# Token blocks of 512 instead of 448, and streaming tiles laid on multiples of 128 bytes

## The chip, the core and the metric

The kernel runs on one core of a Trainium2 chip. The metric is the time of one execution in microseconds of the device. TensorE (PE) multiplies matrices into PSUM; ScalarE (ACT) and VectorE (DVE) work between PSUM and the on-chip memory SBUF; SyncE (SP) issues transfers.

## What is computed

An attention over 49 agents, then two feed-forward layers, for 12480 tokens of 128 channels, in fp32:

```python
def _attn_ref(q, k, v, agents):
    scale = 1.0 / np.sqrt(q.shape[-1])
    def sm(a, b):
        s = scale * (a @ b.transpose(0, 2, 1))
        ...                                     # softmax over the last axis
    agent_v = sm(agents, k) @ v
    return sm(q, agents) @ agent_v              # q is (1, 12480, 128), agents (1, 49, 128)

def _moe_ref(x, w_in, w_out, s, b):             # w_in (128, 2048), w_out (2048, 128)
    r = np.maximum(x @ w_in, 0.0)
    return (s * (r * r) + b) @ w_out

def _moe2_ref(x, w_in, w_out):                  # the second layer, same shapes
    h = np.maximum(x @ w_in, 0.0)
    return h * h @ w_out
```

## The kernel before

**Two halves of each number.** To keep fp32 accuracy with the fast fp32r matmuls, each operand is held as a high half and a low half (names end in `h` and `l`), and a product is two or three matmuls: low by high, high by low, high by high. The weights are decoded into halves on ACT and DVE (`w_decode`, in small portions that `fill` deals out; the table `FILL_L` says how many portions each of the first 22 steps gets).

**The head** (0 to 77 us) reads k and v, forms the agents' values, and folds them into the first layer's weights: `M` is agent values times `w_in` (`m_piece`, L385, 512 columns at a time). L507 streams `wo` past a matrix of ones to get its column sums (`colsum`, 512 columns).

**The loop.** The tokens are cut into blocks. `cut(4, BP)` with `BP = 112` makes 27 blocks of 4 × 112 = 448 tokens and one of 384. A block takes 8 steps (`NPR`), each for two of the 16 chunks of the hidden 2048. A step holds 22 matmuls of one block's width: `up1` (L595) 4, X by `M`; `up2` (L605) 6, y by `wi2`; `down` (L621) 6 and 6, g by `wo` and by `wo2`. The four parts belong to different steps of different blocks (`LAG = 2`, `L2 = 11` steps later), so that PE always has something to do while ACT squares the hidden values (L584, L585 in `hidden`) and DVE splits them into `gh` and `gl` (L125, L126 in `split`). A matmul has two operands in SBUF: the weights, 128 columns that are loaded (PEld) while the matmul ahead still runs, and the streaming tile, one column after another (X, `yh`, `yl`, `gh`, `gl`, and for the scores `qh`, `ql`).

**Around the loop.** Once in a block, in fixed steps of it (`QS`), the queries of the next block are turned into X: `q_scores_T` (L214, two matmuls that stream `ql` and `qh` past `aS`), `q_back` (L229, two transposes), exponent, norm, and `q_stack` (L260, two transposes). q itself is loaded three blocks ahead through SP's queue: the first three blocks directly, later ones channel by channel or, every fourth (`TURN`), in 32 × 32 squares that DVE turns. The result leaves through the same queue.

**Where tiles lie.** Nothing sets an address outright. Pools take space in the order in which they are opened, tiles in a pool in the order of the code, each rounded up to 32 bytes of a partition. `const` holds `ident`, `aT`, `s_sb`, the weights, then the small tiles, a filler `apart` and X; the pool `qp` follows with q, `mx`, `e`, `sm`; the other pools after it. In the built programs this gives (byte of a partition, modulo 512; all weights of a kind, and all buffers of a tile, have the same):

| streaming tile, weights | before: tile, weights | distance modulo 512 | after: tile, weights | distance |
|---|---|---|---|---|
| X, M (L595) | 384, 416 | 480 | 128, 128 | 0 |
| y, wi2 (L605) and g, wo, wo2 (L621) | 64, 416 | 160 | 128, 128 | 0 |
| ql, aS (L214) | 64, 416 | 160 | 128, 128 | 0 |
| qh, aS (L214) | 384, 416 | 480 | 128, 128 | 0 |
| wo, ones_r (L507) | 416, 384 | 32 | 128, 128 | 0 |
| M, av (L385) | 416, 416 | 0 | 128, 128 | 0 |

Of the kernel before, what the change touches and what calls it, by code (L numbers as in the profile page):

```python
# [9 lines left out]
F32 = mybir.dt.float32  # L10
F32R = mybir.dt.float32r
# [4 lines left out]
AX = mybir.AxisListType  # L16

P = 128
BP = 112
SQ = 32  # L20
LAG = 2
WC = 512
# [23 lines left out]
def tile_agent_attention_two_moe(  # L46
# [15 lines left out]
    _, N, C = q.shape  # L62
# [5 lines left out]
    GAP = 64  # L68
    KS = GAP + NA

    def cut(rows, most=P):

        pieces, t = [], 0
        while N - t >= rows * most:
            pieces.append((t, most, rows))
            t += rows * most
        if t < N:
            left = N - t
            p = next(x for x in range(min(most, left), 0, -1) if left % x == 0 and left // x <= rows)
            pieces.append((t, p, left // p))  # L80
        return pieces

    blocks = cut(4, BP)
    kblocks = cut(8)
    NT = sum(j for _, _, j in kblocks)

# [5 lines left out]

    const = ctx.enter_context(tc.tile_pool(name="const", bufs=1))
    qp = ctx.enter_context(tc.tile_pool(name="qp", bufs=2))
    ps_h = ctx.enter_context(tc.tile_pool(name="ps_h", bufs=2, space=bass.MemoryType.PSUM))
    ps_y = ctx.enter_context(tc.tile_pool(name="ps_y", bufs=1, space=bass.MemoryType.PSUM))
    ps_m = ctx.enter_context(tc.tile_pool(name="ps_m", bufs=1, space=bass.MemoryType.PSUM))
# [2 lines left out]
    def small(name):  # L100

        flip[0] = (flip[0] + 1) % (flip[1] + 1)
        return ps_m.tile([P, 512], F32, tag=f"m{flip[0]}", name=name)

    ident = const.tile([P, P], F32, name="ident")
    aT = const.tile([P, GAP], F32, name="aT")
    s_sb = const.tile([P, 1], F32, name="s_sb")
    M = [const.tile([P, DFF], F32R, name=f"M{x}") for x in "hl"]
    wo = [const.tile([P, NCH, C], F32R, name=f"wo{x}") for x in "hl"]
    wi2 = [const.tile([P, DFF], F32R, name=f"wi2{x}") for x in "hl"]  # L110
# [2 lines left out]
    sTs = [const.tile([KS, 256], F32, name=f"sT{i}") for i in range(2)]  # L113
    aS = const.tile([P, P], F32R, name="aS")
    av = [const.tile([P, P], F32R, name=f"av{x}") for x in "hl"]
    b_sb = const.tile([P, 1], F32, name="b_sb")
    y1_bias = const.tile([P, 1], F32, name="y1_bias")
    const.tile([P, 104], F32, name="apart")
    Xs = [const.tile([P, 512], F32R, name=f"X{i}") for i in range(2)]
    ones_r = const.tile([P, P], F32R, name="ones_r")  # L120
    halves = (0, slice(0, NA)), (1, slice(GAP, KS))

    def split(dst, src, eng_lo, copy=nc.vector.tensor_copy):
# [5 lines left out]
    q_raw, qT, q_sT, q_e, q_st, X = {}, {}, {}, {}, {}, {}  # L129

    def tokens_of(x, t):

        t0, p, j = blocks[t]
        return x[t0:t0 + p * j, :].rearrange("(j p) c -> p j c", j=j)

    def squares_of(x, t, a, e, g):

        t0 = blocks[t][0]
        return x[t0 + a:t0 + e, g * SQ:(g + 1) * SQ].rearrange("(b p) c -> p b c", p=SQ)

    def squares(x, a, e, g):

        return x[g * SQ:(g + 1) * SQ, a:e].rearrange("p (b c) -> p b c", c=SQ)

    def q_load(t):
        t0, p, j = blocks[t]
        q_raw[t] = qp.tile([P, 512], F32, tag="q_raw", name="q_raw", bufs=3)
        if t < DIRECT:
            nc.sync.dma_start(out=q_raw[t].rearrange("p (j c) -> p j c", c=C)[:p, :j], in_=tokens_of(q, t))
        else:  # L150
            if t % TURN:
                with nc.allow_non_contiguous_dma(reason="channels on the partitions"):
                    nc.sync.dma_start(out=q_raw[t][:, :p * j], in_=q[t0:t0 + p * j, :].rearrange("t c -> c t"))
            else:
                for g in range(P // SQ):
                    nc.sync.dma_start(out=squares(q_raw[t], 0, p * j, g), in_=squares_of(q, t, 0, p * j, g))
# [8 lines left out]
    def q_transpose(t):  # L165
        _, p, j = blocks[t]
        n = p * j
        raw = q_raw.pop(t)
        if t < DIRECT:
            ps = small("ps_q")  # L170
            for i in range(j):
                nc.tensor.transpose(
                    out=ps[:, i * p:(i + 1) * p], in_=raw[:p, i * C:(i + 1) * C], identity=ident[:p, :p]
                )
            qT[t] = qp.tile([P, 512], F32, tag="qh", name="qT")
            nc.scalar.copy(qT[t][:, :n], ps[:, :n])
        else:
            hi = qp.tile([P, 512], F32R, tag="qh", name="qh")
            lo = qp.tile([P, 512], F32R, tag="ql", name="ql")
            nc.scalar.copy(hi[:, :n], raw[:, :n])  # L180
            qT[t] = (hi, lo, raw)

# [205 lines left out]
    with tc.manual_schedule():  # L388

        with tc.tile_pool(name="pre", bufs=1) as pre, tc.tile_pool(name="kp", bufs=2) as kp:  # L390
# [74 lines left out]
            for g in range(NG + 1):  # L465
                if g < NG:
                    k_transpose(g)
                if g and g + KB - 1 < NG:
                    k_load(g + KB - 1)
                if g == 2:  # L470
                    nc.scalar.dma_start(out=s_sb, in_=s.partition_broadcast(P))
                    nc.scalar.dma_start(out=b_sb, in_=b.partition_broadcast(P))
                if g == 9:
                    q_load(0)
                    q_load(1)
                v_upto(min(g - KB, VB))
                fill(FILL_K[g])
                if g:
                    k_scores(g - 1)
                if g > 2:  # L480
                    k_max(g - 2)

            k_max(NG - 1)
            mxk = pre.tile([P, NA], F32, name="mxk")
            nc.vector.reduce_max(mxk, mxa.rearrange("p j n -> p n j"), axis=AX.X)
            q_transpose(0)
            fill(FILL_T)
            ps = small("ps_mt")
# [3 lines left out]
            dm = pre.tile([NA, NA], F32, name="dm")  # L492
            nc.vector.tensor_scalar_mul(dm, ident[:NA, :NA], mt)
            q_transpose(1)
            fill(FILL_T)
            ps = small("ps_mb")
# [10 lines left out]
                    nc.tensor.matmul(out=ps_cs, lhsT=ones_r, rhs=w, start=(n == 0), stop=(n == 2 * NW - 1))  # L507

            def set_bias():
                x = qp.tile([P, 512], F32, tag="ql", name="cs")  # L510
                nc.vector.tensor_tensor(
                    out=x.rearrange("p (m c) -> p m c", c=C),
                    in0=ps_cs.rearrange("p (m c) -> p m c", c=C),
                    in1=ident.rearrange("p (m c) -> p m c", m=1).to_broadcast([P, 512 // C, C]),
                    op=ALU.mult,
                )
                nc.vector.reduce_sum(y1_bias, x, axis=AX.X)
                nc.vector.tensor_mul(y1_bias, y1_bias, b_sb)
# [128 lines left out]
        for st in range(total + L2 + LAG + 1):  # L647
            t, i = divmod(st, NPR)
            if t + 1 < NB and i == QS[2]:
                q_exp(t + 1)  # L650
            if st == NPR:
                set_bias()
# [10 lines left out]
            if t < NB:  # L663
                up1(t, i)
                if i == 0:
                    for u, far in ((t + 2, t + 2 < DIRECT), (t + 3, DIRECT <= t + 3 < NB)):
                        if far:
                            q_load(u)
                if t + 1 < NB:
                    if t + 2 < NB and i == NPR - 2:  # L670
                        q_turn(t + 2)
                    elif t + 2 < NB and i == NPR - 1:
                        q_transpose(t + 2)
                    if i == QS[0]:
                        (q_scores if t + 1 < DIRECT else q_scores_T)(t + 1)
                    elif i == QS[1] and t + 1 >= DIRECT:
                        q_back(t + 1)
                    elif i == QS[3]:
                        q_norm(t + 1)
                    elif i == QS[4]:  # L680
                        q_stack(t + 1)
            t, i = divmod(st - L2, NPR)
            if 0 <= t < NB:
                up2(t, i)
            t, i = divmod(st - LAG, NPR)
# [4 lines left out]
            t, i = divmod(st - L2 - LAG, NPR)  # L690
# [34 lines left out]
```

## Time and profile before

| | us |
|---|---|
| median of 3 runs | 1103.91 (1103.86 to 1104.81) |
| the profiled execution | 1104.85 |
| its span, first to last instruction | 1102.9 |
| PE busy in it | 1084.2 (98%) |
| DVE busy | 954.4 (87%) |
| ACT busy | 952.8 (86%) |

The rows further down are from that one profiled execution. Matmuls overlap in the pipeline, so the duration of one is longer than the distance between two starts, and the end is modelled; distances of starts are read from the timeline and from the chain of waits.

### The profile page before, as it was taken

How to read it: one execution, taken by the hardware profiler on the slowest of the kernel's cores; microseconds unless marked ns; L12 is line 12 of the kernel's file. 1: busy time of each engine (PE TensorE's matmuls, PEld its weight loads, DVE VectorE, ACT ScalarE, POOL GpSimd, SP SyncE). 2: the span in 40 equal slices, each digit the busy share in tenths (PEclk: the TensorE clock that was granted, in tenths of full speed). 3: DMA queues.
4: the chain of work that ended last, by engine and by line, in shares of the span. 5: the costliest groups of instructions: out<-in, count | busy, mean ns of one | idle time of the engine just before them, and what ended most of it. 6: DMA issues, size and time to landing. Idle time of an engine off the chain costs nothing.

```text
span 1102.9 us, 15258 instructions
## 1 busy us (share of the span) xinstructions
PE 1084.2 (98%) x5651; PEld 1010.8 (92%) x5651; DVE 954.4 (87%) x1413; ACT 952.8 (86%) x1201; POOL 12.5 (1%) x36
## 2 busy tenths in 40 slices
PE   8997999999999999999999999999999999999998
PEld 8886999999999999999999999999999999999997
DVE  5889888888888888988889888888888888888876
ACT  5659998989898889988988988898989898889876
POOL 2010000000000000000000000000000000000000
PEclk9899999999999999999999999999999999999999
DMA  9999949983999909999099992799973999800001
GB/s 342 262 195 15 8 11 8 16 20 11 9 14 15 21 9 8 15 16 13 11 15 15 15 8 18 13 15 8 15 20 12 8 15 15 12 9 1 9 9 16
DMA packets 1163202, 34.95 MB, mean 32 GB/s; under 512 B 1145575, under 2 KB 1159544, under 8 KB 1163128
## 3 DMA queue, kind: packets, MB, share of 16 engines
q1 hardware_dynamic: 1160224, 27.57, 104.0%
q0 software_dynamic: 1728, 6.29, 1.8%
q8 instruction: 44, 0.72, 0.4%
q14 instruction: 30, 0.25, 0.2%
q10 hardware_dynamic: 1176, 0.12, 0.1%
HBM read 27.58 MB, written 6.39 MB: 31 GB/s over the span
## 4 chain that ended last, share of the span: by engine, by line
PE 89%; DVE 3%; ACT 2%; issue 1%; DMA 1%; DVEq 0%; ACTq 0%
PE ps_y L621 47%; PE ps_h L605 24%; PE ps_h L595 16%; PE ps_sT L214 1%; DMA raw<-in_moe_w_out_dram 1%; ACT r L584 1%; DVE gl L126 1%; ACT r L585 1%; PE ps_x L260 0%; PE ps_b L229 0%; DVE gh L125 0%; DVE z L313 0%; DVE x L308 0%; DVE S L523 0%; DVE ex L316 0%
## 5 line engine op out<-in xcount | busy, mean ns | idle before, releaser
L126 DVE TENSOR_TENSOR gl<-r,gh 128x896 fp32r<-128x896 f32 (+2 forms) x450 | 487.6, 1083 | 17.1 <-ACT gh L125 1.8
L584 ACT ACTIVATE r<-ps_h 128x896 f32<-128x896 f32 (+2 forms) x450 | 408.5, 908 | 73.4 <-PE ps_h L595 36.3
L585 ACT ACTIVATE r<-r 128x896 f32<-128x896 f32 (+2 forms) x450 | 427.0, 949 | 14.3
L125 DVE CAST gh<-r 128x896 fp32r<-128x896 f32 (+2 forms) x445 | 275.2, 618 | 101.4 <-ACT r L585 98.3
L605 PE MATMUL ps_h<-yh,wi2l 128*128 128x448 f32 (+1 forms) x448 | 167.3, 374 | 0.2 <-ACT r L584 0.2
L595 PE MATMUL ps_h<-X,Ml 128*128 128x448 f32 (+1 forms) x448 | 163.7, 365 | 2.2 <-DVE X L271 1.3
L595 PE MATMUL ps_h<-X,Mh 128*128 128x448 f32 (+1 forms) x448 | 164.1, 366 | 0.0
L621 PE MATMUL ps_y<-gh,wol 128*128 128x448 f32 (+1 forms) x448 | 162.6, 363 | 1.1 <-ACT y L629 1.1
L621 PE MATMUL ps_y<-gl,woh 128*128 128x448 f32 (+1 forms) x448 | 162.3, 362 | 0.6 <-DVE gl L126 0.6
L621 PE MATMUL ps_y<-gl,wo2h 128*128 128x448 f32 (+1 forms) x448 | 162.2, 362 | 0.1
L605 PE MATMUL ps_h<-yl,wi2h 128*128 128x448 f32 (+1 forms) x448 | 162.2, 362 | 0.0
L621 PE MATMUL ps_y<-gh,woh 128*128 128x448 f32 (+1 forms) x448 | 162.1, 362 | 0.0
L605 PE MATMUL ps_h<-yh,wi2h 128*128 128x448 f32 (+1 forms) x448 | 162.0, 362 | 0.0
L621 PE MATMUL ps_y<-gh,wo2l 128*128 128x448 f32 (+1 forms) x448 | 162.0, 362 | 0.0
L621 PE MATMUL ps_y<-gh,wo2h 128*128 128x448 f32 (+1 forms) x448 | 161.9, 361 | 0.0
L595 PEld LDWEIGHTS ps_h<-X,Ml 128*128 128x128 f32 x448 | 84.4, 188 | 9.2 <-issue 2.9
L621 PEld LDWEIGHTS ps_y<-gh,wol 128*128 128x128 f32 x448 | 84.4, 188 | 7.0 <-ACT y L629 1.4
L595 PEld LDWEIGHTS ps_h<-X,Mh 128*128 128x128 f32 x448 | 84.4, 188 | 6.7
L621 PEld LDWEIGHTS ps_y<-gl,woh 128*128 128x128 f32 x448 | 84.2, 188 | 6.4 <-DVE gl L126 0.9
L605 PEld LDWEIGHTS ps_h<-yh,wi2h 128*128 128x128 f32 x448 | 84.1, 188 | 6.2
L605 PEld LDWEIGHTS ps_h<-yh,wi2l 128*128 128x128 f32 x448 | 84.1, 188 | 6.1 <-ACT r L584 0.6
L621 PEld LDWEIGHTS ps_y<-gl,wo2h 128*128 128x128 f32 x448 | 84.1, 188 | 5.8 <-DVE gl L126 0.6
(122 smaller groups left out, 941.6 us busy)
## 6 DMA issues: line engine op xcount, KB each, us to landing
kraw<-in_k_dram SPq DMA_DIRECT2D x12, 512.0 KB, 12.0
v<-in_v_dram SPq DMA_DIRECT2D x12, 512.0 KB, 8.5
out_dram<-o SPq DMA_DIRECT2D x108, 56.0 KB, 1.9
q_raw<-in_q_dram SPq DMA_DIRECT2D x21, 224.0 KB, 36.3
raw<-in_moe_w_out_dram POOLq DMA_DIRECT2D x8, 512.0 KB, 8.6
raw<-in_moe_w_in_dram SPq DMA_DIRECT2D x4, 512.0 KB, 8.8
raw<-in_moe_w_in_dram POOLq DMA_DIRECT2D x4, 512.0 KB, 7.5
q_raw<-in_q_dram SPq DMA_DIRECT2D x24, 56.0 KB, 2.2
```

The lines of the kernel that those rows point to most:

```text
L125: copy(dst[0], src)
L126: eng_lo.tensor_tensor(out=dst[1], in0=src, in1=dst[0].bitcast(F32), op=ALU.subtract)
L214: nc.tensor.matmul(out=ps[:, :n], lhsT=aS, rhs=x[z][:, :n], start=(z == 1), stop=(z == 0))
L584: nc.scalar.activation(r[:, c, :n], ps[:, c, :n], AF.Relu)
L585: nc.scalar.activation(r[:, c, :n], r[:, c, :n], AF.Square)
L595: nc.tensor.matmul(out=ps[:, c, :n], lhsT=M[z][:, sl], rhs=X[t], start=(z == 1), stop=(z == 0))
L605: nc.tensor.matmul(out=ps[:, c, :n], lhsT=w[:, sl], rhs=y[:, :n], start=(z == 0), stop=(z == 2))
L621: nc.tensor.matmul(out=py[t][:, :n], lhsT=wz[:, m], rhs=g[:, c, :n], start=(m == 0 and z == 0), stop=(m == NCH - 1 and z == 2),)
```

## The change

Blocks become as wide as a matmul allows, 4 × 128 = 512 tokens: 23 of them, then one of 384 and one of 320 (`TAIL`). The tiles are laid anew: the small ones go behind the weights, X and the ones ahead of them, another filler follows, and q's tiles get a pool of their own, `qs`, behind the small tiles of `qp`. No other code changes; lines move by up to 5 (L595 becomes L600, L605 L610, L621 L626).

```diff
-BP = 112
+TAIL = [96, 80]
...
-    blocks = cut(4, BP)
+    blocks, left = [], N
+    for p in [P] * (N // (4 * P) - 1) + TAIL:
+        blocks.append((N - left, p, 4))
+        left -= 4 * p
...
     qp = ctx.enter_context(tc.tile_pool(name="qp", bufs=2))
+    qs = ctx.enter_context(tc.tile_pool(name="qs", bufs=2))
...
     ident = const.tile([P, P], F32, name="ident")
-    aT = const.tile([P, GAP], F32, name="aT")
-    s_sb = const.tile([P, 1], F32, name="s_sb")
     M = [const.tile([P, DFF], F32R, name=f"M{x}") for x in "hl"]
...
     av = [const.tile([P, P], F32R, name=f"av{x}") for x in "hl"]
+    ones_r = const.tile([P, P], F32R, name="ones_r")
+    Xs = [const.tile([P, 512], F32R, name=f"X{i}") for i in range(2)]
+    aT = const.tile([P, GAP], F32, name="aT")
+    s_sb = const.tile([P, 1], F32, name="s_sb")
     b_sb = const.tile([P, 1], F32, name="b_sb")
     y1_bias = const.tile([P, 1], F32, name="y1_bias")
-    const.tile([P, 104], F32, name="apart")
-    Xs = [const.tile([P, 512], F32R, name=f"X{i}") for i in range(2)]
-    ones_r = const.tile([P, P], F32R, name="ones_r")
+    const.tile([P, 120], F32, name="apart0")
...
-        q_raw[t] = qp.tile([P, 512], F32, tag="q_raw", name="q_raw", bufs=3)
+        q_raw[t] = qs.tile([P, 512], F32, tag="q_raw", name="q_raw", bufs=3)
...
-            hi = qp.tile([P, 512], F32R, tag="qh", name="qh")
-            lo = qp.tile([P, 512], F32R, tag="ql", name="ql")
+            hi = qs.tile([P, 512], F32R, tag="qh", name="qh")
+            lo = qs.tile([P, 512], F32R, tag="ql", name="ql")
```

In a steady step PE has, before (numbers behind a name are buffers; the shape is that of the output):

```order
L595 MATMUL ps_h_2251<-X_91,Ml 128x448
L595 MATMUL ps_h_2251<-X_91,Mh 128x448
L605 MATMUL ps_h_2268<-yh,wi2l 128x448
L605 MATMUL ps_h_2268<-yl,wi2h 128x448
L605 MATMUL ps_h_2268<-yh,wi2h 128x448
```

and with the change, at the same place:

```order
L600 MATMUL ps_h_2254<-X_90,Ml 128x512
L600 MATMUL ps_h_2254<-X_90,Mh 128x512
L610 MATMUL ps_h_2271<-yh,wi2l 128x512
L610 MATMUL ps_h_2271<-yl,wi2h 128x512
L610 MATMUL ps_h_2271<-yh,wi2h 128x512
```

The sequence is the same and each matmul is 64 columns wider. Where the last block enters the loop, PE has before:

```order
L595 MATMUL ps_h_10247<-X_92,Ml 128x384
L595 MATMUL ps_h_10247<-X_92,Mh 128x384
L605 MATMUL ps_h_10259<-yh,wi2l 128x448
L605 MATMUL ps_h_10259<-yl,wi2h 128x448
L605 MATMUL ps_h_10259<-yh,wi2h 128x448
```

and with the change:

```order
L600 MATMUL ps_h_9318<-X_90,Ml 128x320
L600 MATMUL ps_h_9318<-X_90,Mh 128x320
L610 MATMUL ps_h_9330<-yh,wi2l 128x384
L610 MATMUL ps_h_9330<-yl,wi2h 128x384
L610 MATMUL ps_h_9330<-yh,wi2h 128x384
```

Two narrower blocks run through the end where one did, and the very last is 320 wide.

## Rows read from the trace of the kernel before

**Rows 1.** The page's busy line: engine, busy us, share of the span, instructions.

```profile
PE 1084.2 (98%) x5651; PEld 1010.8 (92%) x5651; DVE 954.4 (87%) x1413; ACT 952.8 (86%) x1201; POOL 12.5 (1%) x36
```

**Rows 2.** Ramp and loop: length, busy us by engine (instructions), clock, DMA share.

```profile
77.40:118.00 40.60, 34.12 (x163) 29.37 (x164) 37.15 (x63) 37.36 (x49) 0.00 (x0) 0.96 1.58 13
118.00:1040.00 922.00, 922.00 (x4637) 859.61 (x4637) 813.85 (x1155) 825.99 (x1019) 0.00 (x0) 1.00 1.11 13
```

**Rows 3.** Chain of waits in order of time, one step: start, us, what.

```profile
995.13 0.82 PE ps_h L595 x4
995.95 1.20 PE ps_h L605 x6
997.15 2.40 PE ps_y L621 x12
999.55 0.82 PE ps_h L595 x4
```

**Rows 4.** The same chain in the last block and the tail.

```profile
1084.00 1.04 PE ps_y L621 x6
1085.04 1.04 PE ps_h L605 x6
...
1092.36 0.50 ACT r L584
...
1097.46 0.63 PE ps_y L621 x2
```

**Rows 5.** PE's groups by form: count, busy us, mean ns, idle before.

```profile
L595 PE MATMUL ps_h<-X,Mh 128*128 128x448 f32 x432 | 158.7, 367 | 0.0
...
L621 PE MATMUL ps_y<-gh,wo2h 128*128 128x448 f32 x432 | 156.6, 362 | 0.0
...
L214 PE MATMUL ps_sT<-ql,aS 128*128 128x448 f32 x24 | 8.8, 367 | 0.0
L214 PE MATMUL ps_sT<-qh,aS 128*128 128x448 f32 x24 | 8.8, 367 | 0.0
```

**Rows 6.** L385, 512 columns: durations min/median/max in ns, first and last start.

```profile
L385 PE MATMUL ps_M<-Ml,avh x4: 389/434/487, 75.1 to 85.8; 128*128 128x512 f32 x4
...
L385 PE MATMUL ps_M<-Mh,avl x4: 389/394/607, 75.3 to 86.1; 128*128 128x512 f32 x4
...
L385 PE MATMUL ps_M<-Mh,avh x4: 388/393/628, 75.5 to 86.5; 128*128 128x512 f32 x4
```

**Rows 7.** L507, 512 columns, the same view.

```profile
L507 PE MATMUL ps_cs<-wol,ones_r x4: 393/398/398, 73.0 to 74.8; 128*128 128x512 f32 x4
```

**Rows 8.** Timeline of PE, L385: start, us, what.

```profile
75.06 0.39 PE L385 MATMUL ps_M<-Ml,avh 128*128 128x512 f32 x1
...
75.75 0.39 PE L385 MATMUL ps_M<-Ml,avh 128*128 128x512 f32 x1
...
76.21 0.39 PE L385 MATMUL ps_M<-Mh,avh 128*128 128x512 f32 x1
```

**Rows 9.** Timeline of PE at the two transposes of a block.

```profile
538.86 0.36 PE L229 MATMUL ps_b<-ident,sT 113*112 113x113 f32 x2
538.99 0.45 PE L605 MATMUL ps_h<-yh,wi2l 128*128 128x448 f32 x1
539.27 0.37 PE L605 MATMUL ps_h<-yl,wi2h 128*128 128x448 f32 x1
...
991.15 0.36 PE L260 MATMUL ps_x<-ident,stack 112*113 112x112 f32 x2
...
991.57 0.36 PE L605 MATMUL ps_h<-yl,wi2h 128*128 128x448 f32 x1
```

**Rows 10.** PE's waits in the ramp: total us, times, longest.

```profile
PE ps_M L385 <- DVE e L194: 2.1, 1, 2.1
```

**Rows 11.** ACT's groups by form, as rows 5.

```profile
L585 ACT ACTIVATE r<-r 128x896 f32<-128x896 f32 x432 | 413.0, 956 | 13.7
L584 ACT ACTIVATE r<-ps_h 128x896 f32<-128x896 f32 x432 | 395.2, 915 | 65.9 <-PE ps_h L595 34.5 <-DVE gl L126 18.3 <-PE ps_h L605 3.1
```

More of the change, by code (lines that the diff above doesn't have):

```diff
@@ L81, in cut @@
         return pieces
-    blocks = cut(4, BP)
+    blocks, left = [], N
+    for p in [P] * (N // (4 * P) - 1) + TAIL:
+        blocks.append((N - left, p, 4))
+        left -= 4 * p
+    assert left == 0 and all(4 * p % (2 * SQ) == 0 for p in TAIL)
     kblocks = cut(8)
@@ L174, in q_transpose @@
                 )
-            qT[t] = qp.tile([P, 512], F32, tag="qh", name="qT")
+            qT[t] = qs.tile([P, 512], F32, tag="qh", name="qT")
             nc.scalar.copy(qT[t][:, :n], ps[:, :n])
         else:
-            hi = qp.tile([P, 512], F32R, tag="qh", name="qh")
-            lo = qp.tile([P, 512], F32R, tag="ql", name="ql")
+            hi = qs.tile([P, 512], F32R, tag="qh", name="qh")
+            lo = qs.tile([P, 512], F32R, tag="ql", name="ql")
             nc.scalar.copy(hi[:, :n], raw[:, :n])
@@ L509, in set_bias @@
             def set_bias():
-                x = qp.tile([P, 512], F32, tag="ql", name="cs")
+                x = qs.tile([P, 512], F32, tag="ql", name="cs")
                 nc.vector.tensor_tensor(
```

## The prediction

> **What bounds the kernel now.** I read the busy line of the page first [rows 1]: PE is busy for 98% of the span, DVE for 87%, ACT for 86%. A busy PE can still be a slow one, so the stretches come next [rows 2]: from 118 to 1040 us PE has no idle time at all and the full clock, while DVE is busy for 814 and ACT for 826 of 922 us. Only in the ramp before it (77.4 to 118) does PE stand still, 34.1 us busy of 40.6, with both other engines above 91%. The chain of waits, in order of time, then shows what one step is made of [rows 3]: four first-layer matmuls (L595), six of L605, twelve of L621, and the next step begins 4.42 us later. So the time is the number of matmuls times the distance from one start to the next, plus a head and a tail. Everything in the sum turns on that distance, which I call the pitch.
>
> **The pitch.** Twelve matmuls of 448 columns take 2.40 us [rows 3], 200.0 ns each. Six of 384 columns take 1.04 us [rows 4], 173.3 ns. The 64 columns between them cost 26.7 ns, 2.4 columns a nanosecond, so 160.0 ns of the 173.3 are columns and 13.3 ns are not; 448 columns give 186.7 and again 13.3. A matmul thus pays 13.3 ns that do not depend on its width. A third width, 512, stands in the trace ahead of the loop, in twelve matmuls of L385 and eight of L507. The modelled durations help here: they are 362 ns where the pitch is 200 [rows 5], that is 162 more, and the shortest 512-wide ones on L385 last 388 and 389 [rows 6], so their pitch is 226 to 227; columns plus 13.3 would be 226.7.
>
> **A placement that costs.** Not all 448-wide matmuls have the 200.0 pitch. Those that stream X last 367 ns on average, those that stream g last 362 [rows 5]; the step of 22 matmuls is 4.42 us and not 4.40 [rows 3], so the four X matmuls cost 5 ns each above the others. The two matmuls that stream q's halves last the same 367 [rows 5] although another weight stands there; the first of them, `ql`, follows X directly and can have inherited its delay, `qh` comes second. On L507, where `wo` streams past the ones, 512 columns last 393 to 398 [rows 7], a pitch of 231 to 236. So there are slow and fast streams, and I set them beside the table of places above: the distance from the streaming tile to the weights, modulo 512 bytes, is 480 for X, 32 for `wo` on L507, 160 for g and y, 0 for M on L385. The first two are slow, the last two are fast. After the change the distance is 0 for all of them.
>
> By the Trainium skill ("TensorE: Matmul & The Clock Gate", What happens when you issue a matmul) the streaming operand and the weight load have read ports of their own, and loading the next weights takes nothing from the running matmul. By that, places would not matter and the 5 ns would stay; the rows leave the question open, since they show two kinds of stream and not the cause.
>
> **The change part by part**, against the profiled execution's 1104.85 us (span 1102.9 and 1.95 around it; the median of the runs shown, 1103.91, is 0.94 lower).
>
> 1. *Fewer, wider matmuls.* 28 blocks of 176 matmuls become 25: 528 fewer. The columns are the same, 12480 tokens, so what goes is the fixed part: 528 × 13.3 ns = **−7.0 us**, all of it on PE, which waits for nobody in the loop. The same page (Back-to-back issue gap) puts the fixed part at 2.5 ns; by that the saving would be 528 × 2.5 = 1.3 us, but the rows at two widths give 13.3.
>
> 2. *X and q no longer slow.* 224 steps × 4.42 − 4.40 = 0.02 us: **−4.5 us** if the distance of 0 is fast, as L385 has it.
>
> 3. *Residue at distance 0.* L385's six matmuls from 75.06 on start 1.15 us apart over five distances [rows 8], 230 ns on average, 3.3 above 226.7; but the later two distances, 75.75 to 76.21, belong to the 388 and 389 of [rows 6], and the earlier ones stand right behind the slow `wo` rows, whose delay may reach into them. The bounds are 0 and 3.3 ns for each of 23 × 176 = 4048 matmuls, 0 to 13.4 us. A long run resembles the end of that row, so I take 0.6 ns: **+2.4 us**.
>
> 4. *What every block costs once.* The turn of the scores, L229, with the restart behind it takes 538.86 to 539.27, 0.41 us, and L260 takes 991.15 to 991.57, 0.42 us [rows 9]. Each includes one ordinary matmul of 0.20, so a block pays 0.43 us; three blocks fewer give −1.3. The turned tiles are 128 instead of 112 wide; if all of the 0.43 grew by a seventh, 25 blocks would pay 1.5 more, if only the columns of the first of each pair did, about 0.6. I take +0.8, net **−0.5 us**.
>
> 5. *The ramp.* PE waits here for DVE [rows 10], which decodes weights and splits g. The decode is the same amount, keyed to the step by `FILL_L`. Each of about ten steps has 512 instead of 448 columns on DVE and ACT, and PE brings a seventh more work into the same stretch. If ACT's 915 and 956 ns [rows 11] grew in proportion and all of it lay on the path, ten steps would add 10 × (131 + 137) = 2.7 us; against it the 34.1 us of PE work [rows 2] take over up to 10 × 10 × 26.7 ns = 2.7 us that PE has to do anyway and that is already counted in the columns. Bounds −3 and +2, taken **−0.4**.
>
> 6. *The tail.* From 1092.36 ACT and DVE pass the last four 384-wide halves between them, and the last two matmuls start at 1097.46 [rows 4], 5.1 us. At 320 wide, between nothing and a sixth of it (0.85) goes: **−0.4 us**.
>
> *ACT and DVE as cover.* A step of 22 matmuls of 512 takes 22 × 226.7 = 4.99 us. ACT needs two of L584 and two of L585; scaled in full proportion that is 2 × (1046 + 1093) = 4.28 us. The shares of rows 2 fall a little, since their fixed parts also come three blocks fewer. They stay hidden. The transfers of q are issued three blocks ahead on SP's queue and carry fewer scattered bytes than before (by the code 16 blocks go channel by channel instead of 19); the outputs behind them in the queue free a buffer two blocks later. Nothing on PE waits for either in the loop. The moved pools change nothing but addresses.
>
> Sum: −7.0 − 4.5 + 2.4 − 0.5 − 0.4 − 0.4 = −10.4. 1104.85 − 10.4 = 1094.4, and 0.94 less for the median: **1093.5 us**. The case runs from 1088.5 (no residue, −3 in the ramp) to 1100.
>
> **The rivals.**
>
> *A multiple of 128 is itself the slow place (ends slower).* In the loop before, X and the high half of q are the only streaming tiles that begin on a multiple of 128, and they are the slow ones [rows 5]; g and y, at 64, are fast. The change puts every streaming tile there. Then each 512-wide matmul runs at the pitch of L507, about 234 [rows 7], 7.5 ns above 226.7: 4048 × 7.5 = +30.4, the 352 narrower ones some 3 ns each, +1.1, and item 2's −4.5 and item 3's +2.4 fall out. −7.0 + 31.5 − 1.3 = +23.2: about 1127. Against it: `wo` on L507 begins 32 off and is slow, M on L385 begins 32 off and is fast, so the streaming tile's own place does not decide alone. It turns the result once the mean excess of a 512-wide matmul is above (7.0 + 4.5 + 1.3) / 4048 = 3.2 ns. Chance 0.18.
>
> *Placement does nothing.* X and q are slow for another reason and stay so; the rest is as fast as before. This is what the skill's rule of separate ports would give here. X's 5 ns grow with the width (L507's 512-wide rows suggest 7 to 7.5), so 736 rows of 7.25 and 64 narrower ones of 3 cost 5.5 instead of 4.5, item 2 becomes +1.0 and item 3 nothing: −7.0 + 1.0 − 1.3 = −7.3, 1096.6. For it: nothing in the trace moves a tile. Against it: `qh` pays the same beside another weight, and fast and slow follow the distances if `ql`'s row is X's delay. Chance 0.18.
>
> *The residue is larger.* With 2.5 to 3.5 ns at distance 0, the upper bound of item 3, the gain is eaten: 1101 to 1106. Chance 0.07.
>
> *The fixed part is itself a cost of the placement* and shrinks. Then some 40 us would go. L385 at distance 0 has it in full. Chance 0.01.
>
> **How the numbers follow.** My forecast has 0.56, placement without effect 0.18, slow at 128 0.18, large residue 0.07, the last 0.01. 0.2% of the median is 2.2 us, about what a measurement of this kernel can tell from no change, so "same" runs from 1101.7 to 1106.1. Faster: 0.56 + 0.18 + 0.01 = 0.75; same 0.07; slower 0.18. The range takes in the forecast's bounds, placement without effect, and a large part of the residue's case: 1088.5 to 1104, with the slow rival outside.
>
> **What would show it.** Right: 4400 loop matmuls; a steady step of 4.98 to 5.02 us; X's modelled duration within 2 ns of g's, both 388 to 390; PE without idle time in the loop. If X's rows last 395 and g's 389, placement did nothing. If all last 395 to 398 and the step is above 5.12 us, the slow rival holds. Wrong in another way: idle time of PE in the loop behind ACT's L584 (line numbers of before), or a ramp more than 3 us longer.

## The result, and the profile after

| us | before | changed |
|---|---|---|
| median | 1103.88 (1103.42 to 1104.81, 4 runs) | 1092.58 (1092.01 to 1093.21, 4 runs) |
| the profiled execution | 1104.85 | 1093.21 |
| its span | 1102.9 | 1091.3 |

The changed kernel takes 0.990 of the time before, with a 95% interval of 0.9885 to 0.9915: 11.3 us less by the medians, 11.6 by the profiled executions.

The busy line of the page, as in [rows 1]:

```profile
PE 1072.5 (98%) x5105; PEld 903.0 (83%) x5105; DVE 933.4 (86%) x1278; ACT 932.8 (85%) x1081; POOL 12.5 (1%) x36
```

PE still bounds. It has 546 instructions fewer than before: the 528 of the loop and 18 of the steps that every block has once.

Ramp and loop, the windows that answer to [rows 2] (length; busy us and instructions of PE, PEld, DVE, ACT, POOL; clock; DMA share; GB/s):

```profile
77.40:118.00 40.60, 34.57 (x152) 27.14 (x151) 36.55 (x60) 37.83 (x45) 0.00 (x0) 0.96 1.60 13
118.00:1040.00 922.00, 921.76 (x4131) 765.00 (x4130) 801.54 (x1028) 814.83 (x909) 0.00 (x0) 1.00 1.05 13
```

PE is idle for 0.24 of 922 us at full clock, and ACT and DVE have lost 11 and 12 us of busy time there. They remain cover.

The chain of waits in a steady step, which answers to [rows 3] (start, length, what):

```profile
538.70 0.91 PE ps_h L600 x4
539.61 1.36 PE ps_h L610 x6
540.97 2.72 PE ps_y L626 x12
543.68 0.91 PE ps_h L600 x4
```

One step takes 4.98 us by these rows. All three parts have the same pitch: 1.36 / 6 and 2.72 / 12 are both 226.7 ns, which is 512 columns at 2.4 a nanosecond plus 13.3. X is no longer the exception that it was in [rows 3].

PE's groups by form, as [rows 5] (count, busy us, mean ns of one, idle before):

```profile
L600 PE MATMUL ps_h<-X,Mh 128*128 128x512 f32 x368 | 143.7, 391 | 0.0
...
L626 PE MATMUL ps_y<-gl,wo2h 128*128 128x512 f32 x368 | 143.3, 389 | 0.0
...
L219 PE MATMUL ps_sT<-qh,aS 128*128 128x512 f32 x20 | 7.8, 389 | 0.0
...
L626 PE MATMUL ps_y<-gl,wo2h 128*128 128x384 f32 x16 | 5.4, 340 | 0.0
L600 PE MATMUL ps_h<-X,Mh 128*128 128x384 f32 x16 | 5.4, 339 | 0.0
```

X, g and q's high half, 367, 362 and 367 before, now lie within 2 ns of each other; X's 391 is 1 above the 388 to 390 that the prediction named as a sign. Some of the 384-wide ones, as the two shown, are a little longer than the 336 that most of them had before; the last section comes back to that.

**Where the 11.6 us went.** I took the starts of all matmuls from the first X to the end, before and after, and split each distance to the next start into its width's floor (columns / 2.4 + 13.33 ns) and what is above. What is above by less than 60 ns I call the excess; more is a restart or a wait. The last column sums to the difference of the two spans, 1102.90 − 1091.27 = 11.63, within the rounding.

| us | before | after | difference |
|---|---|---|---|
| to the first X | 77.41 | 77.01 | −0.4 |
| floors of the loop's matmuls | 980.73 | 973.72 | −7.0 |
| excess of all of them | 4.51 | 1.99 | −2.5 |
| transposes L229 and L260 (now L234, L265) | 6.84 | 6.08 | −0.8 |
| restart right behind those | 4.65 | 4.13 | −0.5 |
| q's matmuls on L214 (now L219) | 10.15 | 9.70 | −0.4 |
| everything else, mostly waits in ramp and tail | 13.46 | 13.69 | +0.2 |
| last matmul's start to the end | 5.15 | 4.95 | −0.2 |

### The profile page after: what moved, and what is told of

The parts are those of the page before. It is cut to its first block, busy times and chain, and to the rows that moved or that the text cites. A ratio compares the mean times of both kernels' runs of the same rounds, so it can differ in the third digit from the quotient of the medians.

```text
span 1091.3 us, 13795 instructions
## 1 busy us (share of the span) xinstructions
PE 1072.5 (98%) x5105; PEld 903.0 (83%) x5105; DVE 933.4 (86%) x1278; ACT 932.8 (85%) x1081; POOL 12.5 (1%) x36
## 4 chain that ended last, share of the span: by engine, by line
PE 92%; DMA 3%; ACT 2%; DVE 1%; SPq 1%; issue 1%; DVEq 0%; ACTq 0%
PE ps_y L626 47%; PE ps_h L610 24%; PE ps_h L600 15%; PE ps_av L545 2%; DMA kraw<-in_k_dram 2%; SPq L154 1%; ACT r L589 1%; PE ps_sT L219 1%; ACT r L590 1%; DMA q_raw<-in_q_dram 1%; PE ps_x L265 0%; PE ps_b L234 0%; DVE gl L131 0%; PE ps_cs L512 0%; DVE gh L130 0%
## 5 line engine op out<-in xcount | busy, mean ns | idle before, releaser
L131 DVE TENSOR_TENSOR gl<-r,gh 128x1024 fp32r<-128x1024 f32 (+3 forms) x402 | 479.8, 1194 | 15.6 <-ACT gh L130 2.0
L589 ACT ACTIVATE r<-ps_h 128x1024 f32<-128x1024 f32 (+3 forms) x402 | 400.7, 997 | 87.5 <-PE ps_h L600 78.5
L590 ACT ACTIVATE r<-r 128x1024 f32<-128x1024 f32 (+3 forms) x402 | 416.6, 1036 | 12.8
L130 DVE CAST gh<-r 128x1024 fp32r<-128x1024 f32 (+2 forms) x397 | 267.5, 674 | 113.6 <-ACT r L590 107.2
L610 PE MATMUL ps_h<-yh,wi2l 128*128 128x512 f32 (+2 forms) x400 | 157.6, 394 | 0.2 <-ACT r L589 0.2
L600 PE MATMUL ps_h<-X,Ml 128*128 128x512 f32 (+2 forms) x400 | 153.9, 385 | 2.1 <-DVE X L276 1.3
L626 PE MATMUL ps_y<-gh,wol 128*128 128x512 f32 (+2 forms) x400 | 154.2, 385 | 1.0 <-ACT y L634 1.0
L626 PE MATMUL ps_y<-gl,woh 128*128 128x512 f32 (+2 forms) x400 | 153.8, 385 | 0.6 <-DVE gl L131 0.6
L626 PE MATMUL ps_y<-gl,wo2h 128*128 128x512 f32 (+2 forms) x400 | 153.9, 385 | 0.1
L610 PE MATMUL ps_h<-yh,wi2h 128*128 128x512 f32 (+2 forms) x400 | 154.0, 385 | 0.0
L600 PE MATMUL ps_h<-X,Mh 128*128 128x512 f32 (+2 forms) x400 | 153.9, 385 | 0.0
L610 PE MATMUL ps_h<-yl,wi2h 128*128 128x512 f32 (+2 forms) x400 | 153.9, 385 | 0.0
L626 PE MATMUL ps_y<-gh,woh 128*128 128x512 f32 (+2 forms) x400 | 153.8, 384 | 0.0
L626 PE MATMUL ps_y<-gh,wo2h 128*128 128x512 f32 (+2 forms) x400 | 153.7, 384 | 0.0
L626 PE MATMUL ps_y<-gh,wo2l 128*128 128x512 f32 (+2 forms) x400 | 153.5, 384 | 0.0
L600 PEld LDWEIGHTS ps_h<-X,Ml 128*128 128x128 f32 x400 | 75.3, 188 | 17.8 <-issue 2.9
L626 PEld LDWEIGHTS ps_y<-gh,wol 128*128 128x128 f32 x400 | 75.4, 188 | 16.3 <-ACT y L634 1.5
L626 PEld LDWEIGHTS ps_y<-gl,woh 128*128 128x128 f32 x400 | 75.3, 188 | 15.8 <-DVE gl L131 1.0
L600 PEld LDWEIGHTS ps_h<-X,Mh 128*128 128x128 f32 x400 | 75.4, 188 | 15.0
L610 PEld LDWEIGHTS ps_h<-yh,wi2h 128*128 128x128 f32 x400 | 75.1, 188 | 14.6
L626 PEld LDWEIGHTS ps_y<-gh,woh 128*128 128x128 f32 x400 | 75.2, 188 | 14.4
L626 PEld LDWEIGHTS ps_y<-gl,wo2h 128*128 128x128 f32 x400 | 75.1, 188 | 14.6 <-DVE gl L131 0.6
```

Source lines behind the costliest of these rows:

```text
L130: copy(dst[0], src)
L131: eng_lo.tensor_tensor(out=dst[1], in0=src, in1=dst[0].bitcast(F32), op=ALU.subtract)
L589: nc.scalar.activation(r[:, c, :n], ps[:, c, :n], AF.Relu)
L590: nc.scalar.activation(r[:, c, :n], r[:, c, :n], AF.Square)
L600: nc.tensor.matmul(out=ps[:, c, :n], lhsT=M[z][:, sl], rhs=X[t], start=(z == 1), stop=(z == 0))
L610: nc.tensor.matmul(out=ps[:, c, :n], lhsT=w[:, sl], rhs=y[:, :n], start=(z == 0), stop=(z == 2))
```

## The experiments

Distance is again that from the streaming tile to the weights it meets, modulo 512 bytes, read from the addresses in each built program. The pitch of a steady step, away from a block's turns (the transposes L229 and L260), is what an experiment is judged by: the total time of a single execution also carries its own head, whose length differed between runs by up to 3 us.

### Each part alone: wider blocks in the old places, and the new places with the old blocks

`e1_width_only` gives the kernel before the new blocks and leaves its layout:

```diff
-BP = 112
+TAIL = [96, 80]
...
-    blocks = cut(4, BP)
+    blocks, left = [], N
+    for p in [P] * (N // (4 * P) - 1) + TAIL:
...
```

> Blocks of 512, 384 and 320, all tiles left where they were (X and qh at distance 480 from the weights modulo 512, y, ql and g at 160). Distance theory: y and g keep 226.7 ns a matmul, X goes to about 234; 736 X matmuls x 7.25 ns = +5.3 on the changed kernel, about 1098 us. Rival 'only multiples of 128 are fast': no stream but X and no weight lies on one, so most 512-wide matmuls are near 234, about 1120 us. Rival 'placement does nothing': 1092.6 us as the changed kernel.

`e2_place_only` gives the changed kernel the old blocks, the same lines the other way round:

```diff
-TAIL = [96, 80]
+BP = 112
...
-    blocks, left = [], N
-    for p in [P] * (N // (4 * P) - 1) + TAIL:
...
+    blocks = cut(4, BP)
```

> Blocks of 448 and 384 as before, tiles laid as in the changed kernel (distance 0 everywhere). Distance theory and 'multiples of 128': X's modelled duration falls from 367 to 362 ns, the step from 4.42 to 4.40 us, 1103.9 - 4.5 = 1099.4 us. Rival 'placement does nothing': 1103.9 us.

Measured: width alone **1118.53 us** (before on that chip 1103.54, ratio 1.0138, interval 1.0123 to 1.0153); places alone **1112.29** (the same before, 1.0077, 1.006 to 1.0094). The chain of `e1_width_only`:

```profile
541.85 2.81 PE ps_y L625 x12
544.66 0.93 PE ps_h L599 x4
```

and of `e2_place_only`, a whole step:

```profile
542.74 2.43 PE ps_y L622 x12
545.17 0.81 PE ps_h L596 x4
545.99 1.22 PE ps_h L606 x6
547.20 2.43 PE ps_y L622 x12
```

In the first, g at distance 160 has 234 ns a matmul, 7.5 above the floor of 226.7; at 448 columns the same distance was on its floor [rows 3]. In the second, everything at distance 0 has 203, 3 above its floor of 200.0, where the changed kernel at distance 0 has none. The excess, summed over the loop as above, is 28.7 and 14.7 us. So **neither part of the change gains by itself**: +15.0 and +8.7 us apart, −11.3 together, and a sum of the two parts would have been 35 us off. My rule by distance alone, which had 160 and 0 as fast places, falls with both runs, and so does the rival in which placement does nothing. The rival "only multiples of 128 are fast" named the first number (about 1120) but not the second, where everything lies on one and is slow; the next pair tests it at 512 columns.

### The place on a multiple of 128, or the distance

`e3_all_plus32` moves every tile of the changed kernel 32 bytes on, so that nothing begins on a multiple of 128 and the distance stays 0:

```diff
+    const.tile([P, 8], F32, name="shift")     # ahead of M
```

> The changed kernel with a filler of 32 bytes ahead of the weights, so that every weight and every streaming tile lies 32 bytes off a multiple of 128, and all distances stay 0. Distance theory: 1092.6 us, step 4.99 us. Rival 'a multiple of 128 is what counts': 512-wide matmuls above 229 ns, 1102 us or more.

`e4_weights_plus32` does that for the weights and puts a second filler ahead of the streaming tiles, which brings these back onto multiples of 128, at distance 480:

```diff
+    const.tile([P, 8], F32, name="shift")     # ahead of M
...
+    const.tile([P, 120], F32, name="back")    # behind the weights
```

> The changed kernel with all weights 32 bytes later and all streaming tiles still on multiples of 128 (distance 480 modulo 512 everywhere). Distance theory: every 512-wide matmul near 234 ns, 1092.6 + 4048 x 7.3 ns + 1 = about 1123 us. Rival 'streams on multiples of 128 are enough': 1092.6 us.

Measured: **1094.22 us** with everything moved (two executions near 1091 and two near 1097; ratio 0.9917, 0.9887 to 0.9948; the chain shown is that of the one of 1090.84) and **1115.11** with the weights moved (1.0109, 1.0094 to 1.0124). The chain of `e3_all_plus32`:

```profile
543.39 2.72 PE ps_y L627 x12
546.11 0.91 PE ps_h L601 x4
```

and of `e4_weights_plus32`:

```profile
545.96 2.80 PE ps_y L628 x12
548.76 0.93 PE ps_h L602 x4
```

In the first all are on the floor of 226.7 although no tile is on a multiple of 128. In the second all streaming tiles are, modulo 512, exactly where the change puts them, only their weights are 32 bytes further, and the matmuls have 233. It is the **pair** that counts: 6.6 ns a matmul hang on where the weights lie relative to the stream. The first run ends the rival "only multiples of 128 are fast"; the prediction's, "a multiple of 128 is itself the slow place", ended with the changed kernel itself, where all lie on one and none is slow. The 1123 us expected of the second run were 8 too many: 7.3 ns on each of 4048 matmuls are 29.6 us, the whole excess in its loop is 26.4, of which the changed kernel has 2.0, and its head is 1.4 us shorter. It also speaks against the rule of the Trainium skill that the prediction weighed ("TensorE: Matmul & The Clock Gate", What happens when you issue a matmul): with read ports of their own, weights and stream should not care about each other's place, and in this kernel they do, by up to 7.5 ns of 234.

### Other distances at both widths

Four single runs of the changed kernel with fillers ahead of X and with y's and g's tiles made wider and used from an offset; two of them with the blocks of 448. The edit of the first, the others differ in the numbers alone:

```diff
+D_Y, D_G = 16, 32
...
+    const.tile([P, 16], F32, name="dx")
...
-    const.tile([P, 120], F32, name="apart0")
+    const.tile([P, 104], F32, name="apart0")
...
-            hi = gp.tile([P, 2, 512], F32R, tag=f"gh{layer}", name=f"gh{layer}")
...
+            hi = gp.tile([P, 1152], F32R, tag=f"gh{layer}", name=f"gh{layer}")
...
+            hi, lo = (x[:, D_G:D_G + 1024].rearrange("p (c n) -> p c n", c=2) for x in (hi, lo))
...
-            hi = ep.tile([P, 512], F32R, tag="yh", name="yh")
...
+            hi = ep.tile([P, 640], F32R, tag="yh", name="yh")[:, D_Y:D_Y + 512]
...
```

X and y at 64, g at 128, 512 columns:

> Blocks of 512; X and y at distance 64, g at 128 from the weights. The two runs before left this picture: a slow matmul takes 64 columns in about 29 ns (512: 233 ns, 448: 203 to 205), and some pairs of width and distance escape to 226.7 and 200.0: 512 at 0, 448 at 160. Theory 'modulo 128': g escapes (226.7), X and y stay near 233; about 1105 us. Theory 'modulo 512': none escapes, about 1120 us.

X and y at 256, g at 384, 512 columns:

> Blocks of 512; X and y at distance 256, g at 384. Modulo 128: all at 226.7, 1093 us. Modulo 256: X and y escape, g near 233, about 1107 us. Modulo 512: none escapes, about 1120 us.

X and y at 160, g at 64, 448 columns:

> Blocks of 448; X and y at 160, where y and g were in the kernel before, but with all tiles on other addresses; g at 64. If distance and width decide and addresses do not, X and y run at 200.0, X too, which was slow at 480. g at 64 unknown: 200.0 or 203 to 205.

X and y at 32, g at 416, 448 columns:

> Blocks of 448; X and y at 32, g at 416; both equal 160 modulo 128. Modulo 128: all at 200.0, 1099 us. Modulo 256 (416 is 160): g at 200.0, X and y at 203 to 205. Modulo 512: both slow, about 1112 us.

The totals were 1108.87, 1106.59, 1105.61 and 1115.49 us, beside 1103.17 for the kernel before on that chip. From each chain y and g of one step (in the third, X ahead of them), in this order; first `s1_512_64_128`:

```profile
546.41 1.37 PE ps_h L613 x6
547.78 2.78 PE ps_y L629 x12
```

`s2_512_256_384`:

```profile
544.94 1.36 PE ps_h L613 x6
546.30 2.79 PE ps_y L629 x12
```

`t1_448_160_64`:

```profile
546.68 0.82 PE ps_h L599 x4
547.50 1.20 PE ps_h L609 x6
548.70 2.41 PE ps_y L625 x12
```

`t3_448_32_416`:

```profile
548.44 1.24 PE ps_h L609 x6
549.68 2.41 PE ps_y L625 x12
```

One expectation of `t1_448_160_64` failed: y at 160 has 200.3, but X at 160 has 204, and so have the first two of g; only from the third on does g settle, at 200.0 on average. So the first matmuls of a run can be slow by what stands ahead of them, here even where both places are on the floor, and a mixed layout doesn't show what X alone would have. I therefore read y (L613, L609) and the end of g (L629, L625) from the distances of starts. With the runs above and below this is the map, in ns a matmul:

| distance | 0 | 32 | 64 | 128 | 160 | 256 | 384 | 416 | 480 |
|---|---|---|---|---|---|---|---|---|---|
| 512 columns, floor 226.7 | 226.7 | – | 229 | 231 | 234 | **226.7** | 233 | – | 233 |
| 448 columns, floor 200.0 | 203 | 206 | **200.0** | – | **200.0** | – | – | 202.5 | 204 to 205 |

(480 at 448 columns is X of the kernel before, in a run of four.) At 512 columns only 0 and 256 of the seven tried are on the floor, so a distance modulo 256 would describe that row; at 448 columns 160 is on the floor and 416, the same modulo 256, is not. No single modulus describes both rows: of the three in the expectations, 128 fails in all three runs that it was put to, 256 holds in the second run and fails in the fourth, 512 holds in the fourth and fails in the second.

### The best place for each width

`u1_448_all_160`: the old blocks with X, y and g all at 160, the place where y and g were before; of the loop's streams only X gets another distance (q's two have 0 here).

```diff
+BP = 112            # and the rest of e2_place_only, with
...
+D_Y, D_G = 40, 40
...
+    const.tile([P, 40], F32, name="dx")
```

> Blocks of 448 with X, y and g all at distance 160 from the weights, which were 200.0 ns a matmul in the kernel before. Theory 'width and distance together decide': the step is 4.40 us, X no longer slow, 1103.9 - 4.5 = 1099.4 us. Rival 'distance 0 or a multiple of 128 is the good place at any width': 1103.9 or more.

`u2_512_all_256`: the changed kernel with all three at 256.

```diff
+D_Y, D_G = 64, 64
...
+    const.tile([P, 64], F32, name="dx")
```

> The changed kernel with X, y and g at distance 256 instead of 0. The mixed run before had X and y at 256 settle at 226.7 after four matmuls. If 256 is as good as 0 at 512 columns: step 4.99 us, 1092.6 us. If only 0 holds for a whole loop: step near 5.13, 1115 us or more.

Measured: **1098.75 us** (before on that chip 1101.95, ratio 0.9973, 0.9964 to 0.9982) and **1091.07** (0.9899, 0.9883 to 0.9916). A whole step of `u1_448_all_160`:

```profile
543.30 0.80 PE ps_h L599 x4
544.10 1.20 PE ps_h L609 x6
545.30 2.40 PE ps_y L625 x12
547.70 0.80 PE ps_h L599 x4
```

and y and g in `u2_512_all_256`:

```profile
544.74 1.36 PE ps_h L613 x6
546.10 2.72 PE ps_y L629 x12
```

The first is the prediction's item 2 alone. X falls from 0.82 to 0.80 us per four, the step from 4.42 to 4.40, and 3.2 us go, not 4.5: the loop's excess falls from 4.5 to 0.9. X's slowness was a matter of place, and this gain could have been had without touching the blocks. The second is on the same floor as the change, and its ratio of 0.9899 stands beside the change's 0.990 with nearly the same interval; it is no better place, only another good one. None of the versions clearly beats the change.

### Narrower tiles in a slow place

`u3_320_slow_place` and `u4_384_slow_place` are `e4_weights_plus32`, all at distance 480, with narrower blocks throughout:

```diff
-    for p in [P] * (N // (4 * P) - 1) + TAIL:
+    for p in [80] * 39:                       # u4: [96] * 32 + [48]
```

> All blocks 320 wide (39 of them), streams at distance 480 as in e4, where 512 columns took 233.3. Rate theory (a badly placed stream takes 64 columns in 29.2 ns, and a matmul lasts the longer of that and columns + 13.3): 320 columns need 145.8 < 146.7, so no loss at all: a step of 3.23 us. Rival 'a bad place costs a fixed 5 to 7 ns a matmul': 152 to 153 a matmul, 3.36 us a step. The total, about 1130 us, is not the point; ACT comes close to being the bound.

> Blocks of 384 (32, and one of 192), streams at distance 480. Rate theory: 384 columns take 175.0 instead of 173.3, step 3.85 us. Rival 'fixed 5 to 7 ns': 179, 3.94 us.

Their totals, 1180.74 and 1129.56 us, say nothing of places: 39 and 33 blocks pay more fixed parts and more turns, and at 320 PE also waits for ACT. The pitch does. PE's timeline of `u3_320_slow_place`, two X matmuls one step apart with 24 matmuls from the one to the other (22 and q's two):

```profile
400.54 0.31 PE L602 MATMUL ps_h<-X,Ml 128*128 128x320 f32 x1
...
404.06 0.31 PE L602 MATMUL ps_h<-X,Ml 128*128 128x320 f32 x1
```

3.52 us / 24 = 146.7 ns, which is 320 / 2.4 + 13.3. The chain of `u4_384_slow_place`:

```profile
549.47 1.04 PE ps_h L612 x6
550.51 2.08 PE ps_y L628 x12
```

2.08 / 12 = 173.3, again the floor. The place that costs a 512-wide matmul 6.6 ns costs a 384-wide or 320-wide one nothing. The floor itself does not go on to any width, though: the last block of that run is 192 wide, for which columns / 2.4 + 13.3 would be 93.3 ns, and six of its matmuls take 0.67 us, 112 ns each:

```profile
1117.02 0.67 PE ps_h L612 x6
```

They lie at 480 too, and no other place was tried at that width, so what holds them is open.

I had a theory in which a slow place lowers the rate at which columns pass once the floor's 13.3 ns no longer cover it; it wanted 175.0 at 384 and falls. A cost of 5 to 7 ns that is fixed for a slow place wanted 179 and falls too.

### What stays open

The runs show that stream and weights disturb each other by place, at which pairs of width and distance, and by how much. They do not show the mechanism: a conflict of the two readers in SBUF fits that the pair decides, but no counter or row shows one, and the map follows no simple rule that I found. Why the first matmuls behind another kind need some time to settle (X in `t1_448_160_64`) is open too.

## Why the prediction was right, point by point

The profiled execution was to take 1094.4 us and took 1093.21.

**Item 1, fewer and wider matmuls: −7.0, measured −7.0.** The floor of columns / 2.4 + 13.3, read before from 384 and 448 columns [rows 3, 4], held at 512, and in the experiments at 320 and 384. The Trainium skill ("TensorE: Matmul & The Clock Gate", Back-to-back issue gap) has a fixed part of 2.5 ns for a matmul by itself; an estimate by that page's figure puts a 512-wide one at 215.8, and the rows have 226.7.

**Item 2, X and q no longer slow: −4.5, measured −3.5 in the steady steps** (excess there 3.59 to 0.14). The 0.02 us a step are right: the 125 steps of the loop before that hold neither q's matmuls nor a transpose have 2.50 us of excess, 20.0 ns each. The mistake is that all 224 steps were to gain it. `u1_448_all_160` shows the term alone, and there the excess falls by 3.6 us: by the whole 20 ns in those 125 steps, by only 10 in the 50 with a transpose (17 before; 7 with X at 160, which stand behind the transpose), and by next to nothing in the ramp. q's own matmuls on L214 gave another 0.2 that the working by steps of 22 had left out (10.15 us where their floors are 9.95; 9.70 after, floors 9.71); the rest of that row is that fewer matmuls and columns go this way.

**Item 3, residue at distance 0: +2.4, measured +1.1, and in another place.** I spread 0.6 ns over 4048 matmuls. The steady step has none; what there is stands behind a block's transposes and q's matmuls (0.80 us in 23 blocks, 0.42 before) and where blocks of different width alternate at the end (0.87, 0.15 before). PE's timeline behind a turn shows the first kind:

```profile
166.76 0.38 PE L265 MATMUL ps_x<-ident,stack 128*113 128x128 f32 x2
166.90 0.48 PE L610 MATMUL ps_h<-yh,wi2l 128*128 128x512 f32 x1
167.22 0.39 PE L610 MATMUL ps_h<-yl,wi2h 128*128 128x512 f32 x1
...
168.38 0.39 PE L626 MATMUL ps_y<-gh,wol 128*128 128x512 f32 x1
168.60 0.39 PE L626 MATMUL ps_y<-gl,woh 128*128 128x512 f32 x1
```

From 167.22 to 168.38 five distances average 232 ns, then they are on the floor. L385 showed the like in [rows 8], where the starts are 228, 232, 231, 227 and 227 ns apart; I took the early ones for a delay that `wo`'s slow place on L507 left behind. After the change that place is at distance 0, and the same five distances (now L390) are 228, 232, 231, 227 and 227 again. Nor is it a matter of distance 0: `u2_512_all_256` has 2.1 us of excess in its loop, as the change has 2.0.

**Item 4, the turns: −0.5, measured −1.3.** Three blocks fewer gave the whole −1.3; the 0.8 us for wider turned tiles did not come. Of the two transposes only L265 takes longer, and what follows it starts hardly later:

```profile
L260 PE MATMUL ps_x<-ident,stack 112*113 112x112 f32 x54 | 9.9, 264 | 1.1 <-DVE stack L251 1.1
...
L229 PE MATMUL ps_b<-ident,sT 113*112 113x113 f32 x48 | 8.6, 260 | 0.0
```

and after:

```profile
L265 PE MATMUL ps_x<-ident,stack 128*113 128x128 f32 x46 | 8.9, 275 | 0.9 <-DVE stack L256 0.9
...
L234 PE MATMUL ps_b<-ident,sT 113*128 113x113 f32 x40 | 7.1, 259 | 0.0
```

L234 lasts 259 ns where L229 lasted 260, L265 275 where L260 lasted 264. From the starts of all that run behind 118 us, a transpose on L234 takes 62.7 ns to the next start where L229 took 63.2, and one on L265 67.2 where L260 took 66.5.

**Item 5, the ramp: −0.4, measured 0.** From the first X to the first y it takes 36.1 instead of 33.4 us, and the floors of PE's work in it grew by 2.7 of these 2.8: the seventh more work per step came, and the waits did not shrink. PE's longest wait there is as in [rows 10]:

```profile
PE ps_M L390 <- DVE e L199: 2.2, 1, 2.2
```

**Item 6, the tail: −0.4, measured about 0.** From the last start to the end 0.2 us went, and the last waits ahead of it are 0.15 longer.

**What cancelled.** Items 2 and 3 together were to give −2.1, and the loop's excess fell by 2.5; the errors of item 4 (−0.8) and of what I had not foreseen (−0.4 on L214, −0.4 in the head) stand against those of items 5 and 6 (together −0.8 forecast, 0.0 in the table). So the sum was closer than its terms, and that is luck. The upper end of the case, 1100, was not worked out: the residue's bound of 13.4 alone would have carried it to 1104.5.

**ACT as cover** was right: L589 and L590 take 1022 and 1062 ns, less than the 1046 and 1093 of full proportion, so between 896 and 1024 columns each grew by 107 and 106 ns, where full proportion wanted 131 and 137:

```profile
L590 ACT ACTIVATE r<-r 128x1024 f32<-128x1024 f32 x368 | 390.8, 1062 | 11.7
L589 ACT ACTIVATE r<-ps_h 128x1024 f32<-128x1024 f32 x368 | 376.2, 1022 | 74.2 <-PE ps_h L600 70.1 <-ACT wo2h L314 0.9 <-DVE gl L131 0.8
```

**The theory behind items 2 and 3 was only half right.** That stream and weights cost by their distance is shown (`e3_all_plus32`, `e4_weights_plus32`). That a distance is fast or slow whatever the width is wrong: 160 is on the floor at 448 and 7.5 ns above at 512; 0 is the reverse. What saved the number is that the evidence for 0, L385, was 512 wide like the loop after the change; the prediction did not ask for that, so it was luck. The evidence for 32, L507, was no evidence. The change puts it at distance 0 and its durations stay about what they were in [rows 7], 393 to 398:

```profile
L512 PE MATMUL ps_cs<-wol,ones_r x4: 393/395/397, 72.6 to 74.4; 128*128 128x512 f32 x4
```

These are short runs that restart behind other work, so they can belong to the settling above, not to a place.

**The rivals.** "A multiple of 128 is the slow place" was turned down by the result; but the price it was given, 7.5 ns on every 512-wide matmul, is nearly paid in `e1_width_only`, for another reason (28.5 us of excess on 4048 of them, 7.0 each). "Placement does nothing" would have given 1096.6 and is refuted by every pair of runs above. "The residue is larger" does not occur at 512 columns; with the old blocks it does, 3 ns in `e2_place_only`. "The fixed part is itself a cost of the placement" is refuted by the floor, which keeps its 13.3 ns at distance 0; its 40 us had no working, all of 4400 × 13.3 ns being 58.5.

## What to carry to other kernels

When the bounding engine shows no idle time, measure the distance from start to start by width and by operand: rows of the same shape that differ by a few nanoseconds point at something that can be moved for nothing, here at the places of two tiles in SBUF. Judge a tile's width and its place together, since a place that is free at one width can cost at another, and an edit of either can be worth nothing or less until the other follows. Take a reference pitch from long, steady runs of matmuls of the very width that is planned, not from short ones behind a restart.

## What the runs showed of the hardware

- In long steady runs an fp32r matmul with a weight load of its own starts columns / 2.4 + 13.3 ns after the one ahead, at the best place tried: 146.7 at 320 columns, 173.3 at 384, 200.0 at 448, 226.7 at 512. At 192 columns, at distance 480 alone, it took 112, more than that line's 93.3.
- Where stream and weights lie relative to each other adds between nothing and 7.5 ns to each at 512 columns, and between nothing and 6 at 448; at 320 and 384 columns the one place tried in long runs, 480, added nothing.
- After a transpose of a few columns the pitch needs about six matmuls of 512 columns to come back to its floor, even at a distance that is free: behind the first, the next five average 5.0, 6.6, 1.0, 2.7 and 2.1 ns above it in the changed kernel. At 448 columns (`u1_448_all_160`) it needs four. Matmuls of 512 columns among narrower ones at the end of the changed kernel stay 4 ns above it on average, and those of 384 columns 2.6; the chain there has 1.07 us for six of 384, where 1.04 is the floor:

```profile
1055.14 1.07 PE ps_h L610 x6
...
1070.65 1.07 PE ps_y L626 x6
```
